# A queue of half tiles for block 1's weights, and two output copies of the first turn on GpSimd, in a transformer block on one core

## The chip, the core and the metric

The kernel runs on one core of one Trainium2 chip. The names of the engines are those of the profile: PE (TensorE matmul; PEld is its weight load), DVE (VectorE), ACT (ScalarE), POOL (GpSimd) and SP (SyncE, which here issues all DMAs, in order; its queue is written SPq). The metric is the device time of one execution in microseconds. Each engine works through its own instructions in order and waits on semaphores for those of others.

## The reference

One transformer block with adaptive layer norm, in float32: 2048 tokens of width 576, 32 heads of width 18, and a feed-forward layer 4608 wide.

```python
mod = (_silu(c) @ w_mod).reshape(c.shape[0], 6, 1, -1)
sa, ca, ga, sb, cb, gb = (mod[:, 0], ...)
h = _layernorm(x) * (1 + ca) + sa
x = x + ga * _A_ref(h, A_wqkv, A_wo)      # qkv, softmax(q k / sqrt(Dh)) v, @ wo
h = _layernorm(x) * (1 + cb) + sb
x = x + gb * _B_ref(h, B_w1, B_w2)        # silu(h @ w1) @ w2
```

## The kernel before

**Split numbers.** A float32 operand of a large product is kept as a high part, rounded to fp32r, and a low part, the rest; a product is three passes (high x high, and the two mixed ones). A weight tile therefore goes through GpSimd once: a cast makes the high part, a subtraction the low one, and the weights that a modulation gate scales (wo by ga, w2 by gb) are multiplied by it first.

**Stages.** The first layer norm and the q, k and v projections come first. Then attention goes over four blocks of 512 queries, each over 8 quads of four heads; one pass over the eight quads is called a turn here. For a quad, an estimate of each row's largest score is gathered from psa with DVE's mx (L755, L757), turned to mt (L777), written by SP to mscr (L782) and read back as two rows of qt (L786), so that the second scores, psb (L805), come out with the maximum subtracted; ACT makes pt from them (exponential, L807), and PE sums pt with v in psv (L842), which ACT evicts (ov, L846). out_b (L860 to L870) normalizes that on DVE and sends it with DMAs on SP to the output rows ou.

What follows attention in a block b runs in the next turn, cut into small pieces between the attention matmuls on PE (post(b); of the last block it runs alone at the end). o_T(kt) makes the split of ou: th (high, ACT, L923) and tl (low, GpSimd L926; for the half tile kt = 4 DVE, L928). proj multiplies by wo; then come the second layer norm, its transposes h_T, and the feed-forward layer in 36 tiles of 128, in chunks of four: mlp1 works on two w1 tiles at a time and ends in g (ACT) and its low part (GpSimd, L1072), mlp2 on four w2 tiles, for four groups of 128 tokens. Each result of proj and mlp2 is added to x in two halves: DVE adds the first, and the second goes over ACT into gt (L950, two buffers) and is added by GpSimd (L951).

**Weights.** Only block 1 (b = 0) splits weights. weights() loads a raw half tile from HBM (L672, three buffers), splits it on GpSimd (L674 to L676) and at its next call sends the finished tile to scratch memory (L665); the later blocks load that (L667). The calls stand where the list of pieces asks for them, as pieces without matmuls: prefetch for wo, w_load and w2_load for w1 and w2.

**Order.** PE's order is written out by the kernel: a loop of steps takes by turns a score matmul, a value matmul or the next piece of the filler (post's list), with a plan of when the other engines will be done (plan.t is its clock in ns, chain and plan.op book work on A, V or G), and an item's need holds it back until then. The other engines' order comes from a scheduler that follows the program's order; after_pe ties an instruction to PE's turn.

Of the kernel before, what the change touches and what calls it, by code (L numbers as in the profile page):

```python
# [60 lines left out]
PVMAX, PVMIN = 5, 3  # L61
QKB = 3
# [28 lines left out]
def f(ap):  # L91
    return ap.bitcast(F32)
# [247 lines left out]
def tile_adaln_block(ctx: ExitStack, tc: tile.TileContext, x, wqkv, wo, w1, w2, c, wfirst, wcol, out):  # L340
# [318 lines left out]
    stores = []  # L659

    def weights(w, src, scr, first, gate=None):

        while stores:
            w_, scr_ = stores.pop()
            nc.sync.dma_start(f(scr_), f(w_))  # L665
        if not first:
            nc.sync.dma_start(f(w), f(scr))  # L667
            return
        n = w.shape[2] // 2
        for cs in (slice(0, n), slice(n, 2 * n)):  # L670
            raw = mp["p"].tile([P, 320], F32, tag="raw", name="raw", bufs=3)[:, :n]
            nc.sync.dma_start(raw, src[:, cs])  # L672
            if gate is not None:
                nc.gpsimd.tensor_tensor(raw, raw, gate[:, cs], op=ALU.mult)  # L674
            nc.gpsimd.tensor_copy(w[:, 1, cs], raw)
            nc.gpsimd.tensor_tensor(w[:, 0, cs], raw, f(w[:, 1, cs]), op=ALU.subtract)  # L676
        stores.append((w, scr))
# [173 lines left out]
    def out_b(i, ov):  # L851
# [15 lines left out]
        chain([("V", 700), ("V", 260), ("V", 460), ("V", 700)], plan.t + 700, None, lambda at: o.update({("at", b): at + 5500}))  # L867
# [24 lines left out]
    def prefetch(b):  # L892
        pool = mp["p"]
        c = ready[b] = {}
        for kt in range(KT):
# [4 lines left out]
            weights(w, wo[:, kt, :], wos[kt], b == 0, ga)  # L900
# [6 lines left out]
    def post(b):  # L907
# [7 lines left out]
        def o_T(kt):  # L915
# [5 lines left out]
            chain([("A", 600)], plan.t, None, lambda at: o.update(th=at + 1500))  # L921
            n = P if kt < 4 else 64
            after_pe(nc.scalar.activation(hi[:n], src[:n], AF.Copy))  # L923
            eng = nc.vector if last and kt % 2 == 0 or kt == 4 else nc.gpsimd
# [5 lines left out]
        def proj(j, part):  # L930
            if part == 0:
                def ops(g, i):
                    kt, a, w = PASS[i]
                    return (c["tl"] if a else c["th"])[:, kt, j * P:(j + 1) * P], c["wo", kt][:, 1 - w, g * HH:(g + 1) * HH]

                c["pp"] = Pair([bank("psp", psA)[:, :HH] for _ in range(2)], ops, 14, not state["tail"])
# [85 lines left out]
        def w_load(i):  # L1022
            c["w1", i] = pool.tile([P, 2, KT * P], F32R, tag="w1", name="w1t", bufs=W1B)
            weights(c["w1", i], w1[i], w1s[i], b == 0)

        def w2_load(i):
            c["w2", i] = pool.tile([P, 2, D], F32R, tag="w2", name="w2t", bufs=5)
            weights(c["w2", i], w2[i], w2s[i], b == 0, gb)
# [15 lines left out]
        def mlp1(i, part):  # L1044
            if part == 0:
# [5 lines left out]

                c["p1"] = Pair([bank("ps1", psA) for _ in range(2)], ops, 14, not state["tail"], short=not last)
# [22 lines left out]
        def mlp2(i0, j, part):  # L1075
            if part == 0:
# [3 lines left out]

                c["p2"] = Pair([bank("ps2", psF)[:, :HH] for _ in range(2)], ops, 3 * CH, not state["tail"])
# [17 lines left out]
        fl.add(0, lambda: w_load(0))  # L1099
        fl.add(0, lambda: w_load(1))  # L1100
        fl.add(0, lambda: w2_load(0))
        if EARLY:
# [5 lines left out]
        def add_mlp1(i, w2n=()):  # L1108

            for part in range(NG):  # L1110
                fl.add(MMC * len(GR[not last][part]), lambda part=part: mlp1(i, part), need={0: pair_need, NG // 2: half_need}.get(part))
                for p_, n in w2n:
                    if p_ == part:
                        fl.add(0, lambda n=n: w2_load(n))
                if part in (0, 2) and i + 2 < NFT:
                    fl.add(0, lambda n=i + 2 + part // 2: w_load(n))

        def add_mlp2(i0, add):
            for j in range(NST):
                for part in range(len(G2)):  # L1120
                    add(MMH * len(G2[part]), lambda j=j, part=part: mlp2(i0, j, part), None, {0: pair_need, len(G2) // 2: half_need}.get(part))

        add_mlp1(0)
        for i0 in range(0, NFT, CH):
            if i0 + CH < NFT:
                add_mlp1(i0 + 2, [(NG // 2, i0 + 1)])
                add_mlp1(i0 + CH, [(0, i0 + 2), (0, i0 + 3)])
                add_mlp2(i0, fl.add)
                fl.add(0, lambda i=i0 + CH: w2_load(i))
            else:  # L1130
                add_mlp1(i0 + 2, [(1, i0 + 1), (2, i0 + 2), (3, i0 + 3)])
# [366 lines left out]
    while now < 2 * (total + LEAD) or pend or later:  # L1498
# [5 lines left out]
        run_later()  # L1504
        fill.free()
# [109 lines left out]
```

## Time and profile before

| | |
|---|---|
| runs, median (lowest to highest) | 2426.76 us (2426.68 to 2430.24) |
| the profiled execution: its own time, its span | 2421.15 us, 2419.3 us |
| PE busy | 2326.0 us, 96% |
| DVE busy | 1777.0 us, 73% |
| ACT busy | 1483.1 us, 61% |
| POOL busy | 629.8 us, 26% |
| mean granted clock of PE | 0.989 |

The profile is of one execution, which is why its time is not the median. A row of the profile names a line, an engine, an operation and out<-in, with the number of instructions and the time; in brackets stands how long the engine had been idle before, and what released it. The clock that PE is granted is given as a share of full speed. PE's share of 96% is an average over stages with different limits, so the prediction reads it turn by turn.

### The profile page before, as it was taken

Reading aid. Unit: us, or ns where it says so; the run is one execution under the profiler, and the core shown is the slowest. Engines: PE = TensorE matmul, PEld = TensorE weight load, DVE = VectorE, ACT = ScalarE, POOL = GpSimd, SP = SyncE. Lnnn points to the kernel's source line nnn. Section 1 sums busy time; section 2 is a strip of 40 time slices with the busy share of each in tenths; the row PEclk is TensorE's granted clock in tenths of the full one; section 3 lists DMA queues with packets and bytes.
Section 4 is the critical chain, followed back from the end, with each engine's and each line's share of the span. In section 5 each row is a group of like instructions: output and inputs, shape, how many; then the busy total and the mean of one; then the engine's idle time right before and its main releaser. Section 6 shows DMA issues by size and latency. Waiting matters only on the chain.

```text
span 2419.3 us, 52050 instructions
## 1 busy us (share of the span) xinstructions
PE 2326.0 (96%) x19844; PEld 1599.3 (66%) x19844; DVE 1777.0 (73%) x3110; ACT 1483.1 (61%) x2736; POOL 629.8 (26%) x766
## 2 busy tenths in 40 slices
PE   6999999998999999989999999999999999989999
PEld 4874444434567767666667677776676777678998
DVE  8768989886877778767887887888887887134333
ACT  5247777775666767666676776776776677722121
POOL 5201011113665665663211111112211111110000
PEclk9999999999999999999999999999999999999999
DMA  7455555454566666665555554554644554336563
GB/s 252 162 175 173 164 175 179 158 156 154 193 212 201 208 213 210 205 210 173 194 176 179 181 167 157 171 183 140 207 163 162 185 177 163 120 104 233 197 210 117
DMA packets 201472, 432.99 MB, mean 179 GB/s; under 512 B 31362, under 2 KB 67618, under 8 KB 201226
## 3 DMA queue, kind: packets, MB, share of 16 engines
q1 hardware_dynamic: 201226, 429.68, 53.9%
q8 instruction: 158, 2.59, 0.5%
q14 instruction: 88, 0.72, 0.1%
HBM read 338.54 MB, written 86.33 MB: 176 GB/s over the span
## 4 chain that ended last, share of the span: by engine, by line
PE 80%; DMA 6%; DVE 6%; POOL 3%; ACT 3%; issue 2%; SPq 0%; ACTq 0%; POOLq 0%; DVEq 0%
PE ps L485 23%; PE psv L842 17%; PE psa L755 12%; PE ps L479 10%; PE psb L805 8%; PE psqk L590 3%; DMA raw<-in_w 3%; DVE mx L757 2%; PE psv L485 2%; PE psp L485 1%; ACT pt L807 1%; PE psqk L485 1%; PE psv L1288 1%; POOL w1t L676 1%; PE psqk L1288 1%
## 5 line engine op out<-in xcount | busy, mean ns | idle before, releaser
L757 DVE TENSOR_REDUCE mx<-psa 128x1 f32<-128x512 f32 x2048 | 1321.3, 684 | 319.3 <-PE psb L805 168.8
L807 ACT ACTIVATE pt<-psb 128x512 f32<-128x512 f32 x2048 | 1131.6, 598 | 495.0 <-PE psb L805 306.5
L805 PE MATMUL psb<-qt,kb 56*128 56x512 f32 x2048 | 753.7, 425 | 37.8 <-ACT pt L807 23.9
L755 PE MATMUL psa<-ka,qt 54*128 54x512 f32 x2016 | 699.6, 415 | 6.3 <-DVE mx L757 5.2
L755 PEld LDWEIGHTS psa<-ka,qt 54*128 54x128 f32 x2016 | 337.0, 186 | 293.2 <-DVE mx L757 196.2
L842 PE MATMUL psv<-pt,vt 128*32 128x512 f32 x4096 | 512.7, 604 | 2.3 <-ACT ov L846 1.7
L485 PE MATMUL ps<-w2t,g 64*128 64x288 f32 x4992 | 413.8, 295 | 2.5 <-ACT gt L950 2.4
L805 PEld LDWEIGHTS psb<-qt,kb 56*128 56x128 f32 x2048 | 354.1, 185 | 85.9 <-ACT pt L807 56.4
L485 PEld LDWEIGHTS ps<-w2t,g 64*128 64x128 f32 x4992 | 386.9, 188 | 35.8 <-DVE mx L757 10.1
L485 PE MATMUL ps<-hh,w1t 64*128 64x512 f32 x1944 | 371.4, 394 | 2.6 <-DVE x L947 1.6
L485 PEld LDWEIGHTS ps<-hh,w1t 64*128 64x128 f32 x1944 | 220.6, 186 | 39.8 <-DVE mx L757 9.2
L842 PEld LDWEIGHTS psv<-pt,vt 128*32 128x32 f32 x4096 | 99.4, 109 | 215.8 <-issue 208.9
L1072 POOL TENSOR_TENSOR g<-etmp,g 128x512 fp32r<-128x512 f32 x108 | 137.9, 1298 | 393.9 <-ACT g L1071 336.2
L951 POOL TENSOR_TENSOR x<-x,gt 128x288 f32<-128x288 f32 x116 | 92.7, 801 | 408.6 <-ACT gt L950 408.6
L485 PE MATMUL ps<-hl,w1t 64*128 64x512 f32 x864 | 197.5, 392 | 0.6 <-POOL hl L412 0.6
L947 DVE TENSOR_TENSOR x<-ps,x 128x288 f32<-128x288 f32 x184 | 83.9, 456 | 124.4 <-PE ps L479 76.5
L479 PE MATMUL ps<-w2t,g 128*128 128x288 f32 x960 | 133.5, 299 | 7.4 <-ACT g L1071 5.9
L479 PEld LDWEIGHTS ps<-w2t,g 128*128 128x128 f32 x960 | 131.1, 191 | 9.9 <-ACT g L1071 6.3
L485 PEld LDWEIGHTS ps<-hl,w1t 64*128 64x128 f32 x864 | 105.3, 186 | 11.0 <-POOL hl L412 1.1
L1068 ACT ACTIVATE eq<-ps 128x512 f32<-128x512 f32 x36 | 21.6, 600 | 146.3 <-PE ps L479 146.3
L479 PE MATMUL ps<-hh,w1t 128*128 128x512 f32 x360 | 106.9, 390 | 0.5 <-DVE hh L414 0.5
L1069 DVE SCALAR_TENSOR_TENSOR etmp<-etmp 128x512 f32<-128x512 f32 x108 | 77.1, 747 | 22.9 <-ACT etmp L1068 22.3
(144 smaller groups left out, 2076.6 us busy)
## 6 DMA issues: line engine op xcount, KB each, us to landing
w1t<-w1s SPq DMA_DIRECT2D x108, 640.0 KB
w2t<-w2s SPq DMA_DIRECT2D x108, 576.0 KB
kb<-kscr SPq DMA_DIRECT2D x512, 108.0 KB
ka<-kscr SPq DMA_DIRECT2D x504, 108.0 KB
w1s<-w1t SPq DMA_DIRECT2D x36, 640.0 KB
w2s<-w2t SPq DMA_DIRECT2D x36, 576.0 KB
vt<-vscr SPq DMA_DIRECT2D x32, 608.0 KB
qt<-qscr SPq DMA_DIRECT2D x128, 108.0 KB
```

Source lines behind the costliest of these rows:

```text
L479: mm(self.ps[late], lhsT=lhsT, rhs=rhs, start=(i == 0), stop=(i == self.n - 1))
L485: done = mm(self.ps[g], lhsT=lhsT[rows], rhs=rhs[rows], start=(s == 0), stop=(s == self.end))
L590: mm(qk_ps[0], lhsT=w[b][:, kt, :], rhs=(hTl if a else hTh)[:, kt, n * 512:(n + 1) * 512], start=(i == 0), stop=(i == 13))
L755: mm(ps, lhsT=t["q"][64 * j:64 * j + 54, hp, stt * P:(stt + 1) * P], rhs=t["a" if ("a", kc, hp) in t else "b", kc, hp][64 * j:64 * j + 54, ...
L757: return lambda: nc.vector.tensor_reduce(t["mx"][:, 2 * j + hp, stt, kc:kc + 1], ps, axis=AX.X, op=ALU.max)
L805: state["pe"] = mm(ps, lhsT=t["b", kt // 4, hp][64 * e:64 * e + 56, kt % 4 * P:(kt % 4 + 1) * P], rhs=t["q"][64 * e:64 * e + 56, hp, :], s ...
L807: nc.scalar.activation(t["P"][kt, hp][:, e, :], ps, AF.Exp, scale=SCALE)
L842: mm(t["ps"][32 * h:32 * h + 32, :], lhsT=t["v"][:, c0:c0 + 32], rhs=t["P"][kt, h // 2][:, h % 2, :], start=(kt == 0), stop=(kt == NKT - 1 ...
L947: nc.vector.tensor_add(c["x1"][j][:, hs], ps, c["x1"][j][:, hs])
L951: nc.gpsimd.tensor_add(c["x1"][j][:, hs], c["x1"][j][:, hs], t)
L1069: nc.vector.scalar_tensor_tensor(t, t, 1.0, u, op0=ALU.add, op1=ALU.mult)
L1072: (nc.vector if last else nc.gpsimd).tensor_tensor(g[:, 1, :], t, f(g[:, 0, :]), op=ALU.subtract)
```

## The change

weights() no longer loads and splits in block 1. It enters an ask in a queue, a w1 tile ahead of w2 tiles of which nothing has been loaded. serve(), called once per step of the main loop, does at most one store, one split of a half and one load of a half: a load when fewer than three halves are under way and 1500 ns (w1) or 2000 ns (gated) of the plan have passed since the last, a split when 5000 ns have passed since its load, a store 4000 ns after the tile's second split. Load and split are tied to PE's turn. settle() makes what is still missing before the first matmul that reads it.

The requests are moved: four w1 tiles, and in block 1 four w2 tiles too, stand right behind the projection (before two and one), and later ones a few parts further on in mlp1 and mlp2. In block 1's o_T the casts of kt = 3 and 4 and the low part of kt = 4 go to GpSimd, and the plan's time at which ou has landed is put 1000 ns later.

```diff
+EACH, LAND, STORE = (1500, 2000), 5000, 4000
...
-    stores = []
-    def weights(w, src, scr, first, gate=None):
-        while stores:
-            w_, scr_ = stores.pop()
-            nc.sync.dma_start(f(scr_), f(w_))
+    asks, flight, stores = [], [], []
+    last_load = [0]
+    def weights(key, w, src, scr, first, gate=None):
         if not first:
             nc.sync.dma_start(f(w), f(scr))
             return
-        n = w.shape[2] // 2
-        for cs in (slice(0, n), slice(n, 2 * n)):
-            raw = mp["p"].tile([P, 320], F32, tag="raw", name="raw", bufs=3)[:, :n]
-            nc.sync.dma_start(raw, src[:, cs])
-            if gate is not None:
-                nc.gpsimd.tensor_tensor(raw, raw, gate[:, cs], op=ALU.mult)
-            nc.gpsimd.tensor_copy(w[:, 1, cs], raw)
-            nc.gpsimd.tensor_tensor(w[:, 0, cs], raw, f(w[:, 1, cs]), op=ALU.subtract)
-        stores.append((w, scr))
+        ask = {"key": key, "w": w, "src": src, "scr": scr, "gate": gate, "n": w.shape[2] // 2, "at": 0, "halves": [0, 1]}
+        i = len(asks)
+        while key[0] == "w1" and i and asks[i - 1]["key"][0] == "w2" and len(asks[i - 1]["halves"]) == 2:
+            i -= 1
+        asks.insert(i, ask)
+    def load_half():
+        ask = asks[0]
+        h, n = ask["halves"].pop(0), ask["n"]
+        raw = mp["p"].tile([P, 320], F32, tag="raw", name="raw", bufs=3)[:, :n]
+        after_pe(nc.sync.dma_start(raw, ask["src"][:, h * n:h * n + n]))
+        flight.append((plan.t, ask, h, raw))
+        last_load[0] = plan.t
+        if not ask["halves"]:
+            asks.pop(0)
+    def split_half():
+        _, ask, h, raw = flight.pop(0)
...
+        if gate is not None:
+            after_pe(nc.gpsimd.tensor_tensor(raw, raw, gate[:, cs], op=ALU.mult))
+            nc.gpsimd.tensor_copy(hi, raw)
+        else:
+            after_pe(nc.gpsimd.tensor_copy(hi, raw))
+        nc.gpsimd.tensor_tensor(w[:, 0, cs], raw, f(hi), op=ALU.subtract)
+        if h:
+            stores.append((plan.t + STORE, w, ask["scr"]))
...
+    def serve():
+        if stores and stores[0][0] <= plan.t:
+            store_one()
+        if flight and flight[0][0] + LAND <= plan.t:
+            split_half()
+        if asks and len(flight) < 3 and last_load[0] + EACH[asks[0]["gate"] is not None] <= plan.t:
+            load_half()
...
-        chain([...], plan.t + 700, None, lambda at: o.update({("at", b): at + 5500}))
+        chain([...], plan.t + 700, None, lambda at: o.update({("at", b): at + (5500 if b else 6500)}))
...
             n = P if kt < 4 else 64
-            chain([("A", 600)], plan.t, None, lambda at: o.update(th=at + 1500))
-            after_pe(nc.scalar.activation(hi[:n], src[:n], AF.Copy))
-            eng = nc.vector if last and kt % 2 == 0 or kt == 4 else nc.gpsimd
+            if b == 0 and kt > 2:
+                o["th"] = plan.t + 2200 * (kt - 2)
+                after_pe(nc.gpsimd.tensor_copy(hi[:n], src[:n]))
+            else:
+                chain([("A", 600)], plan.t, None, lambda at: o.update(th=at + 1500))
+                after_pe(nc.scalar.activation(hi[:n], src[:n], AF.Copy))
+            eng = nc.vector if last and kt % 2 == 0 or b and kt == 4 else nc.gpsimd
...
-        fl.add(0, lambda: w_load(0))
-        fl.add(0, lambda: w_load(1))
+        for i in range(4):
+            fl.add(0, lambda i=i: w_load(i))
         fl.add(0, lambda: w2_load(0))
+        if b == 0:
+            for i in range(1, 4):
+                fl.add(0, lambda i=i: w2_load(i))
...
             if i0 + CH < NFT:
-                add_mlp1(i0 + 2, [(NG // 2, i0 + 1)])
-                add_mlp1(i0 + CH, [(0, i0 + 2), (0, i0 + 3)])
-                add_mlp2(i0, fl.add)
-                fl.add(0, lambda i=i0 + CH: w2_load(i))
+                w2s_ = [(0, w2_load, i0 + 1), (4, w2_load, i0 + 2), (9, w2_load, i0 + 3)] if i0 or b else []
+                if i0 == 0:
+                    w2s_ += [(1, w_load, 4), (3, w_load, 5)]
+                add_mlp1(i0 + 2, *w2s_)
+                add_mlp1(i0 + CH, (6, w_load, i0 + 6), (11, w_load, i0 + 7))
+                add_mlp2(i0, fl.add, (2, w_load, i0 + 8), (9, w_load, i0 + 9), (18, w2_load, i0 + 4))
...
         run_later()
+        serve()
         fill.free()
```

**How the instructions move.** In the rows below stand line, operation, out<-in, the tile's size and, behind an x, a count; a number behind a name tells tiles of one name apart and differs between the kernels. First GpSimd, around the adds to x in a second-layer chunk of the second turn (in which block 1's post-attention work runs); before:

```order
L1072 TENSOR_TENSOR g<-etmp,g 128x512 x2
L676 TENSOR_TENSOR w1t<-raw,w1t 128x320
L675 CAST w1t<-raw 128x320
L674 TENSOR_TENSOR raw<-raw,gb 128x288
L676 TENSOR_TENSOR w1t<-raw,w1t 128x320
L674 TENSOR_TENSOR raw<-raw,gb 128x288
L951 TENSOR_TENSOR x_6582<-x_6582,gt 128x288
L674 TENSOR_TENSOR raw<-raw,gb 128x288
L951 TENSOR_TENSOR x_6584<-x_6584,gt 128x288
```

and with the change:

```order
L1125 TENSOR_TENSOR g<-etmp,g 128x512 x2
L695 CAST w1t<-raw 128x320 x2
L696 TENSOR_TENSOR w1t<-raw,w1t 128x320 x2
L1003 TENSOR_TENSOR x_6528<-x_6528,gt 128x288
L695 CAST w1t<-raw 128x320
L696 TENSOR_TENSOR w1t<-raw,w1t 128x320
L695 CAST w1t<-raw 128x320
L696 TENSOR_TENSOR w1t<-raw,w1t 128x320
L695 CAST w1t<-raw 128x320
L696 TENSOR_TENSOR w1t<-raw,w1t 128x320
L1003 TENSOR_TENSOR x_6530<-x_6530,gt 128x288
```

Before, raw halves of w2 are multiplied by the gate right ahead of each x add. With the change whole splits (cast, subtract) stand there, those of halves that SP loads further ahead.

Second SP, around one quad's max row in the second turn, mscr and its reload qt; before:

```order
L665 DMA w1s<-w1t 128x1280
L672 DMA raw<-in_w 128x288 x2
L665 DMA w1s<-w1t 128x1280
L672 DMA raw<-in_w 128x320
L724 DMA kb_84<-kscr 54x512 x2
L724 DMA ka_83<-kscr 54x512 x2
L724 DMA kb_85<-kscr 54x512 x2
L665 DMA w2s<-w2t 128x1152
L672 DMA raw<-in_w 128x320
L782 DMA mscr<-mt 128x32
L672 DMA raw<-in_w 128x320
L786 DMA qt<-mscr 2x32x32 x2
```

and with the change:

```order
L703 DMA w1s<-w1t 128x1280
L679 DMA raw<-in_w 128x320
L771 DMA kb_86<-kscr 54x512 x2
L771 DMA ka_83<-kscr 54x512
L771 DMA kb_87<-kscr 54x512
L703 DMA w1s<-w1t 128x1280
L771 DMA ka_83<-kscr 54x512
L679 DMA raw<-in_w 128x320
L771 DMA kb_87<-kscr 54x512
L829 DMA mscr<-mt 128x32
L679 DMA raw<-in_w 128x320
L833 DMA qt<-mscr 2x32x32 x2
```

The rows keep their mixture: a raw load stands between mscr and the reload in both, and the stores of finished tiles (w1s, w2s) come a few places further ahead of mscr.

Third the first turn's output copies. On ACT before:

```order
L807 ACTIVATE pt_2038<-psb 128x512 x2
L807 ACTIVATE pt_2030<-psb 128x512 x2
L807 ACTIVATE pt_2031<-psb 128x512 x2
L923 ACTIVATE th<-ou 128x512
L923 ACTIVATE th<-ou 64x512
L807 ACTIVATE pt_2032<-psb 128x512 x2
L807 ACTIVATE pt_2033<-psb 128x512 x2
```

and on GpSimd with the change:

```order
L693 CAST wo_6527<-raw 128x288
L977 TENSOR_TENSOR tl<-ou,th 128x512 x3
L696 TENSOR_TENSOR wo_6527<-raw,wo_6527 128x288
L971 CAST th<-ou 128x512
L971 CAST th<-ou 64x512
L977 TENSOR_TENSOR tl<-ou,th 128x512
L979 TENSOR_TENSOR th<-ou,th 64x512
```

The two th copies have left ACT's exponentials (pt), and stand on GpSimd with the subtractions behind them, the last of which (th<-ou,th) was DVE's.

43 lines of the change are left out of this document (31 added, 12 removed).

## The prediction

> **What bounds the kernel now.** I split the span at the last evictions of output quads 8, 16, 24 and 32, which bound the second to fourth turn over the eight head quads, and read each stretch (columns: window, its length, then busy us and count of PE, PEld, DVE, ACT and POOL, granted PE clock, DMA share, GB/s):
>
> ```profile
> 564.30:1119.50 555.20, 519.92 (x4816) 361.85 (x4816) 423.57 (x713) 360.58 (x661) 329.43 (x455) 0.97 0.61 198
> 1119.50:1631.10 511.60, 506.85 (x5008) 362.86 (x5004) 418.97 (x720) 362.21 (x667) 93.96 (x94) 1.00 0.53 176
> 1631.10:2130.80 499.70, 494.37 (x4804) 343.62 (x4806) 351.95 (x611) 347.78 (x644) 93.03 (x93) 1.00 0.48 160
> ```
>
> All three are bound by PE (94, 99 and 99% busy). The first of them, the second turn, in which block 1's post-attention work runs and its weights are split, has PE idle for 555.2 - 519.9 = 35.3 us, against 4.8 and 5.3 in the others, and a clock under 1.00. Only that excess can be won; the change leaves the later two in their order. So I looked next for the half-clock stretches of the second turn, and for the PE instructions that stood idle before them:
>
> ```profile
> 577.70:587.90 10.20, 3.69 (x15) 1.59 (x17) 2.36 (x3) 3.31 (x6) 1.26 (x1) 0.50 0.51 177
> 704.00:707.30 3.30, 3.30 (x29) 3.30 (x26) 1.18 (x2) 1.25 (x3) 1.34 (x2) 0.50 0.33 108
> 762.00:765.30 3.30, 3.30 (x28) 3.30 (x26) 1.76 (x3) 1.40 (x3) 2.14 (x3) 0.50 0.60 197
> 874.70:878.00 3.30, 3.30 (x27) 3.30 (x27) 1.95 (x3) 1.59 (x3) 2.85 (x5) 0.50 0.60 200
> 973.60:980.40 6.80, 5.54 (x25) 1.98 (x27) 0.44 (x1) 1.00 (x2) 5.99 (x7) 0.50 0.58 184
> 1045.30:1052.10 6.80, 4.59 (x31) 4.62 (x33) 1.44 (x3) 1.68 (x3) 2.60 (x5) 0.50 0.40 124
> ...
> 584.21 1.27 PE L805 MATMUL psb<-qt,kb 56*128 56x512 f32 x2 [9.07 <-ACT pt L807]
> 703.02 0.50 PE L805 MATMUL psb<-qt,kb 56*128 56x512 f32 x1 [2.70 <-ACT pt L807]
> 760.35 0.50 PE L805 MATMUL psb<-qt,kb 56*128 56x512 f32 x1 [1.19 <-ACT pt L807]
> 815.72 0.50 PE L805 MATMUL psb<-qt,kb 56*128 56x512 f32 x1 [0.87 <-ACT pt L807]
> 872.92 0.53 PE L485 MATMUL ps<-w2t,g 64*128 64x288 f32 x4 [2.36 <-ACT gt L950]
> 974.86 0.76 PE L805 MATMUL psb<-qt,kb 56*128 56x512 f32 x1 [4.85 <-issue]
> 1047.51 1.09 PE L805 MATMUL psb<-qt,kb 56*128 56x512 f32 x2 [6.86 <-DMA qt<-mscr]
> ...
> PE psb L805 <- issue: 6.3, 2, 4.8
> ```
>
> Six half-clock stretches, each beside one of these stalls; half of a stretch is lost. (The last row says that a second stall of the sixth one's kind was 6.3 - 4.85 = 1.5.) They have three causes.
>
> **A, the first turn's output copies.** ACT holds two th copies that wait for the transfer of ou, and its exponentials queue behind them:
>
> ```profile
> 582.24 0.63 ACT L923 ACTIVATE th<-ou 128x512 fp32r<-128x512 f32 x1 [8.36 <-DMA ou<-ov]
> ```
>
> PE stood 9.07 at 584.21; with 10.2 / 2 = 5.1 of clock that is **14.2 us**.
>
> **B, splits ahead of the x adds.** The stalls at 703, 760, 816 and 873 are one chain: GpSimd waits for a raw half tile to land, behind it stands the x add, behind that ACT's gt eviction (two gt buffers), behind that PE:
>
> ```profile
> 870.88 0.79 POOL L674 TENSOR_TENSOR raw<-raw,gb 128x288 f32<-128x288 f32 x1 [1.61 <-DMA raw<-in_w]
> 871.63 0.79 POOL L951 TENSOR_TENSOR x<-x,gt 128x288 f32<-128x288 f32 x1
> ...
> ACT gt L950 <- POOL x L951: 16.2, 5, 4.7
> ```
>
> 2.70 + 1.19 + 0.87 + 2.36 = 7.1 of idle, and three stretches of 3.3 / 2 = 5.0: **12.1 us**.
>
> **C, late max rows.** SP issues its DMAs in order, and waits for GpSimd's splits before raw loads and stores (the second turn's rows, the last one the third's):
>
> ```profile
> SPq L672 <- POOL w1t L676: 70.9, 25, 5.9
> SPq L665 <- POOL w1t L676: 33.2, 30, 3.9
> SPq L786 <- DMA mscr<-mt: 26.5, 8, 5.4
> SPq L665 <- POOL w2t L676: 24.8, 20, 4.2
> ...
> SPq L786 <- DMA mscr<-mt: 16.8, 8, 3.6
> ```
>
> The first, second and fourth sum to 128.9 us. What queues behind them is a quad's max row, which goes out to mscr and back as two rows of qt before that quad's next scores may run:
>
> ```profile
> 955.86 0.21 DVE L777 STREAM_TRANSPOSE mt<-ms 128x32 f32<-128x32 f32 x1
> 965.64 1.07 SPq L782 DMA_DIRECT2D mscr<-mt  x1
> ...
> 1026.86 0.21 DVE L777 STREAM_TRANSPOSE mt<-ms 128x32 f32<-128x32 f32 x1
> 1038.72 0.34 SPq L782 DMA_DIRECT2D mscr<-mt  x1
> 1044.49 1.38 SPq L786 DMA_DIRECT2D qt<-mscr  x2
> ```
>
> mt was ready 965.64 - 956.07 = 9.6 and 1038.72 - 1027.07 = 11.7 us before its store was issued; the stalls that followed were 4.85 and 6.86, each about 4.8 shorter than the lateness. So a store on time ends them. Sum: 4.85 + 1.5 + 6.86 = 13.2, and 2 x 6.8 / 2 = 6.8: **20.0 us**.
>
> **The change part by part.** *o_T.* The copies of kt 3 and 4 leave ACT for GpSimd, the kt-4 subtraction leaves DVE for it. GpSimd's rows of the second turn (count | busy us, mean ns | idle before), with its longest wait for a raw half and a stretch of 60 us for PE's pace:
>
> ```profile
> L676 POOL TENSOR_TENSOR w1t<-raw,w1t 128x320 fp32r<-128x320 f32 x72 | 63.4, 892 | 0.2
> L676 POOL TENSOR_TENSOR w2t<-raw,w2t 128x288 fp32r<-128x288 f32 x72 | 59.4, 837 | 0.4
> L674 POOL TENSOR_TENSOR raw<-raw,gb 128x288 f32<-128x288 f32 x72 | 59.4, 825 | 80.8 <-DMA raw<-in_w 80.2 <-PE psb L805 0.4
> L1072 POOL TENSOR_TENSOR g<-etmp,g 128x512 fp32r<-128x512 f32 x34 | 43.5, 1297 | 0.3 <-ACT g L1071 0.3
> L675 POOL CAST w1t<-raw 128x320 fp32r<-128x320 f32 x72 | 33.7, 476 | 80.0 <-DMA raw<-in_w 61.2 <-PE ps L485 11.7 <-PE psb L805 4.8
> L675 POOL CAST w2t<-raw 128x288 fp32r<-128x288 f32 x72 | 30.2, 442 | 18.8 <-PE ps L485 18.2
> ...
> L990 POOL CAST h<-etmp 128x512 fp32r<-128x512 f32 x1 | 0.6, 612 | 0.0
> ...
> POOL raw L674 <- DMA raw<-in_w: 80.2, 54, 5.2
> ...
> 840.00:900.00 60.00, 57.64 (x541) 42.48 (x540) 45.89 (x76) 39.29 (x73) 40.07 (x54) 0.97 0.63 205
> ```
>
> Two casts at 0.61, one subtraction already there and one new (each 1.30, by the 512-column row of g) make 3.8 us behind the landing, where ACT, POOL and DVE shared them before. The wait for the landing stays, but on GpSimd, behind which only block 1's weights queue; ACT goes on with exponentials, and the plan gives the projection 1 us more. Bounds: nothing of the stall left (gain 14.2), or PE short of other work for the 9.07 less the pt matmuls it can now feed (gain 5). I keep 3 of idle and one short stretch (1.7), since the projection still starts after the same transfer: gain **9.5**.
>
> *The queue.* No matmul, byte or GpSimd operation is dropped: a w1 half costs 0.476 + 0.892 = 1.37 us, a gated w2 half 0.825 + 0.442 + 0.837 = 2.10, before as after. What moves is when. In the two listings of the instructions' order a split's first operation now stands a median of 43 PE instructions behind its raw load's place, before 12; at 60.00 us for 541 of them that is 4.8 us against 1.3, near the longest landing wait above (5.2). So the 80.2 + 61.2 us in which GpSimd waited for landings mostly go, and with them the engine's lateness on which B hangs: x adds stand behind splits whose data are there. Bounds 0 to 12.1 (a loss is rival 2's); I take **11**, leaving one short wait.
>
> SP in turn waits for GpSimd only where a raw buffer or a store asks too early: a raw load is issued by the plan's clock, at most three halves under way, a store 4 us behind its split by the plan. That takes most of the 128.9 us out of SP's queue. But one raw load still stands between mscr and its reload in four of eight quads, and a w1 or w2 store a few places ahead of mscr. Bounds 0 to 20.0; I leave 4 for one late row: **16**.
>
> *What comes closer.* The second-layer weights of the first chunk go right behind the projections: 8 x 1.37 + 8 x 2.10 = 27.8 us of GpSimd against loads spaced 8 x 1.5 + 8 x 2.0 = 28. It is hidden by LN2, whose GpSimd work is small; uncovered, each us is one of PE. And weights are ready later: w1 tile 5's last subtraction stands 18 PE instructions (2.0 us) ahead of its first matmul, before 94 or more; the last w2 half of a typical chunk 56 to 61 (6.2 to 6.8 us), before 165 or more. Bounds 0 (all on time) to 8 chunks times several us (rival 2); I take one stall of 1.8 with a 3.3-us stretch at half speed, **-3.5**, for the tightest of them. The small waits of the turn that hang on the same queues give +1.
>
> Sum: 9.5 + 11 + 16 - 3.5 + 1 = **34**. The profiled execution took 2421.15, so 2387 there; it lies 2426.76 - 2421.15 = 5.6 under the median of the runs, so the predicted time is 2393.
>
> [...]
>
> **Rivals.** (1) *The max rows stay late.* Their transfers, not SP's waits, may hold them: mscr took up to 5.4 us to land against 3.6 in the third turn, behind weight stores and raw loads that all stay, in part in the same places. Against it: the lateness of 9.6 and 11.7 was before the issue. If 12 of C's 16 stay lost, the gain is 22: 2405.
>
> [...]
>
> (2) *Weights come too late: slower.* In the 6.2 to 6.8 us that the last w2 half has, GpSimd may have a w1 half (1.37), two g subtractions (1.30 each) and the half itself (2.10) to do: 6.1. The margin is nil, so a raw half that lands r late is r of PE in each of eight chunks, with some 1.7 of clock. At r = 2.6 the 8 x 4.3 = 34 eat the gain; at the longest landing wait, 5.2, they cost 55: 2427 + 21 = 2448. For it: all chunks share the pattern. Against it: the split is placed after the planned landing, g and splits rarely meet at once, and GpSimd has 555 - 329 = 226 us free.
>
> (3) *Throughput, not order, is the limit*, and the stalls only move: no change, 2427. Against it: GpSimd was busy 59% and DMA 61%.
>
> **How the numbers follow.** Forecast (gain 24 to 46, 2381 to 2403) 0.60; rival 1 (2403 to 2415) 0.18; rival 2 0.16; rival 3 0.06. 46 is A, B and C whole. About 0.2% (4.9 us) is what a measurement here can tell from no change. Faster is the first two and a third of rival 3: 0.80; same 0.04; slower 0.16. The range of eight in ten runs from 2380 up to the milder end of rival 2, at r = 1.5 and its clock, 8 x 3.2 = 26 against 34, which is 2419, and a little beyond: 2422.
>
> **What would show it.** A: no idle over 3 us near the start of the second turn, ACT without a th copy there, GpSimd waiting for ou. B: no ACT gt behind a POOL x of over 1 us. C: SP's waits for GpSimd below 40 us, mscr within 2 us of mt, no psb waiting for qt. Rival 1: mscr on time but landing over 5 us later. Rival 2: PE's layer matmuls waiting for w2t or w1t subtractions at the chunks. The second turn should shrink from 555.2 to about 521, the next two stay within 2 us. I am wrong if the turn's half-clock stretches stay near six, or a new wait repeats by the chunk.

## The result and the profile after

The change made the kernel faster, by less than half of what was forecast: 2412.47 us median (2407.57 to 2414.7, 4 runs) against 2427.97 (2426.68 to 2430.24), a ratio of 0.9932, 95% interval [0.9914, 0.9951]; run again on another chip, 0.9952 [0.9933, 0.9972]. The forecast was 34 us, measured are 15.5. The profiled execution took 2407.57 us, 13.6 less than that of before.

The windows of the three turns with the change (columns as in the prediction), bounded by the same evictions:

```profile
563.70:1095.20 531.50, 512.76 (x4816) 355.90 (x4816) 423.60 (x712) 359.57 (x658) 330.81 (x449) 0.99 0.63 204
1095.20:1615.70 520.50, 509.46 (x5008) 365.23 (x5004) 418.38 (x720) 362.49 (x667) 101.92 (x106) 0.99 0.53 177
1615.70:2117.30 501.60, 496.24 (x4804) 343.81 (x4804) 351.94 (x612) 347.60 (x643) 93.11 (x93) 1.00 0.48 160
```

The second turn is 555.2 - 531.5 = 23.7 us shorter, but the third is 520.5 - 511.6 = 8.9 longer, and the fourth 1.9. A turn that I took as untouched pays part of the bill: the last chunk's waits, below, lie in it. The PE instructions that stood idle longest, from the timeline:

```profile
580.28 0.53 PE L486 MATMUL psp<-wo,th 64*128 64x288 f32 x4 [1.84 <-POOL th L971]
582.40 0.61 PE L486 MATMUL psp<-wo,tl 64*128 64x288 f32 x2 [1.59 <-POOL tl L977]
...
606.86 0.49 PE L802 MATMUL psa<-ka,qt 54*128 54x512 f32 x1 [1.80 <-DVE mx L804]
...
662.88 0.50 PE L486 MATMUL ps<-hh,w1t 64*128 64x512 f32 x2 [1.18 <-POOL w1t L695]
666.53 0.77 PE L486 MATMUL ps<-hh,w1t 64*128 64x512 f32 x1 [3.14 <-POOL w1t L696]
...
1108.74 0.53 PE L486 MATMUL ps<-w2t,g 64*128 64x288 f32 x4 [2.00 <-POOL w2t L696]
1112.28 0.61 PE L486 MATMUL ps<-w2t,g 64*128 64x288 f32 x2 [3.00 <-POOL w2t L693]
```

The old stalls are gone. New ones wait for GpSimd at three places: the output copies (580), w1 tiles 4 and 5 (663 to 667), and the last chunk's w2 (1109 to 1112). Behind each of them stands a stretch at half clock:

```profile
581.30:588.00 6.70, 5.10 (x35) 4.76 (x37) 1.29 (x2) 1.08 (x2) 2.31 (x2) 0.50 0.26 88
666.60:669.90 3.30, 3.30 (x16) 2.65 (x18) 1.09 (x2) 0.60 (x2) 3.17 (x3) 0.50 0.72 293
1110.40:1117.10 6.70, 4.56 (x32) 4.24 (x34) 1.36 (x2) 1.08 (x2) 2.62 (x4) 0.50 0.43 172
```

Where B and C had been, PE stood idle for 8.8 and 12.1 us before the change (first view), and for 0.5 and 2.9 with it (second):

```profile
690.00:905.00 215.00, 206.18 (x1942) 146.77 (x1938) 164.42 (x271) 142.01 (x260) 134.26 (x187) 0.98 0.63 205
955.00:1085.00 130.00, 117.90 (x1115) 84.21 (x1114) 92.65 (x151) 80.35 (x147) 79.77 (x109) 0.95 0.63 206
```

```profile
690.00:890.00 200.00, 199.50 (x1961) 143.91 (x1959) 165.33 (x272) 142.23 (x261) 128.56 (x177) 1.00 0.65 212
940.00:1060.00 120.00, 117.11 (x1141) 84.33 (x1139) 95.59 (x156) 83.03 (x152) 82.56 (x111) 1.00 0.68 219
```

Since both kernels leave 19844 PE records in nearly the same order, the start of the n-th of them can be compared. The table gives it for this and later runs, in us against the profile of before (negative is earlier), each counted from its own 3450th, because starts drift by a few us ahead of the second turn, as SP's loads of qt at 567.42 us in the full change and at 570.76 in "w1 first, no front" show (the text calls the n-th record the n-th matmul):

```
n-th PE record            3500   3700   4200   4300   8300   8700    last
before, at us            554.8  594.6  658.3  671.9 1111.8 1154.4
full change               -0.6   -3.6   -0.4   +4.9  -24.3  -15.3   -13.5
full change again         -0.6   -2.5   -1.5   +6.3  -23.8  -13.8   -14.1
copies only               -0.6   +0.4   +5.9   +5.9   +0.3   +1.4    +1.6
queue only                -0.6   -1.3   -1.4   +6.5  -22.3  -13.5   -11.1
first chunk later         -0.6   -2.4   -1.6   +6.3  -18.1   -9.2    -7.6
last chunk fast           -0.6   -4.0   -1.1   +6.6  -22.2  -21.0   -21.0
w1 asked first            -0.6   -2.1   -0.6   +3.6  -26.3  -25.1   -24.9
w1 first, no front        -0.6   -2.8   -2.2   -2.7  -27.4  -25.3   -21.6
new places, no queue      -0.6   +1.0   +7.6   +7.1   -5.3   -5.4    -4.8
no landing time           -0.6   -8.2   -7.2   -7.5  +82.3  +93.0   +94.7
store at once             -0.6   -6.2   -0.5   -0.8  -19.4  -17.7   -16.6
queue, old places         -0.6   -2.2   +0.4   +0.6 +134.3 +141.0  +142.6
w1 first, no copies       -0.6   -1.8   -0.6   -0.8  -25.2  -24.0   -21.4
wo at once                -0.6   -9.1   -7.4   -7.5  -34.1  -32.2   -28.4
wo at once, no copies     -0.6   -5.3   -2.4   -2.7  -27.1  -25.9   -24.1
w1 first, again           -0.6   -2.3   -1.3   -1.2  -26.8  -24.6   -24.6
```

Columns 3500 to 4200 hold term A and the layer norm, 4200 to 4300 the wait for w1, 4300 to 8300 terms B and C, 8300 to 8700 the last chunk. With the change: A +0.2 (forecast -9.5), w1 +5.2, B and C -29.2 (-27), the last chunk +9.0; the forecast had +3.5 for all that comes closer, and -1 for small waits. Two terms are wrong; the sum of B and C is not. The 6700th matmul (931.0 us before) lies between B's stalls and C's two long ones: up to it -16.1 of the 29.2 had come, behind it -13.1.

### The profile page after: what moved, and what is told of

It is laid out like the page before. It is cut to its first block, busy times and chain, and to the rows that moved or that the text cites. A ratio compares the mean times of both kernels' runs of the same rounds, so it can differ in the third digit from the quotient of the medians.

```text
span 2405.8 us, 52151 instructions
## 1 busy us (share of the span) xinstructions
PE 2323.4 (97%) x19844; PEld 1596.2 (66%) x19844; DVE 1775.2 (74%) x3109; ACT 1482.1 (62%) x2734; POOL 637.5 (26%) x769
## 4 chain that ended last, share of the span: by engine, by line
PE 84%; DVE 7%; DMA 4%; ACT 3%; POOL 2%; issue 1%; SPq 0%; ACTq 0%; POOLq 0%; DVEq 0%
PE ps L486 25%; PE psv L889 18%; PE psa L802 13%; PE ps L480 10%; PE psb L852 8%; PE psqk L591 3%; DVE mx L804 3%; PE psp L486 2%; PE psv L486 2%; DMA raw<-in_w 1%; ACT pt L854 1%; PE psqk L486 1%; PE psv L1350 1%; PE psqk L1350 1%; PE psp L480 1%
```

## The experiments

Their times (median us, and the ratio to the kernel before on the same chip):

| run | median | ratio, 95% interval |
|---|---|---|
| copies only | 2429.94 | 1.0022 [1.0009, 1.0035] |
| queue only | 2415.14 | 0.9965 [0.9952, 0.9977] |
| first chunk later | 2419.07 | 0.9972 [0.9963, 0.9981] |
| last chunk fast | 2405.65 | 0.9921 [0.9906, 0.9936] |
| full change again | 2413.24 | 0.9952 [0.9933, 0.9972] |
| w1 asked first | 2401.15 | 0.9897 [0.9877, 0.9917] |
| w1 first, no front | 2399.91 | 0.9890 [0.9864, 0.9917] |
| new places, no queue | 2421.50 | 0.9983 [0.9967, 0.9998] |
| no landing time | 2518.61 | 1.0381 [1.0359, 1.0404] |
| store at once | 2401.70 | 0.9907 [0.9889, 0.9925] |
| queue, old places | 2568.85 | 1.0594 [1.0576, 1.0613] |
| w1 first, no copies | 2400.50 | 0.9885 [0.9865, 0.9906] |
| wo at once | 2396.43 | 0.9884 [0.9870, 0.9898] |
| wo at once, no copies | 2398.67 | 0.9894 [0.9878, 0.9909] |
| w1 first, no front, again | 2402.58 | 0.9908 [0.9894, 0.9922] |

"No front" means that the first chunk's w2 tiles 1 to 3 are not asked for right behind the projection; "no copies" means without the o_T edit. "W1 first, no copies" and the two runs "wo at once" have no front either.

### The two halves of the change

The kernel before with the new lines of o_T alone, and the full change with the old ones (the lines are those of the diff ahead of the prediction):

```diff
-            eng = nc.vector if last and kt % 2 == 0 or kt == 4 else nc.gpsimd
+            if b == 0 and kt > 2:               # copies only; queue only is this reversed
+                after_pe(nc.gpsimd.tensor_copy(hi[:n], src[:n]))
...
+            eng = nc.vector if last and kt % 2 == 0 or b and kt == 4 else nc.gpsimd
```

> The kernel before with the o_T edit alone (th copies of kt 3 and 4 and the kt-4 subtraction on GpSimd, the plan's times with it). Theory: PE no longer stands 9.07 us for pt, but what it wins is some 3 us at 595 us of the profile and goes again in the layer norm behind it (waits for DVE and for the projection's operands), so that from about 660 us on PE is level with the kernel before: within 1.5 us there, and a time within 2 us of before. Rival: the copies are worth what I forecast (9.5 us) and it was the queue's later weights that took it back in the full change: then PE is 5 to 10 us ahead at 660 us and the time is that much shorter.

> The full change without its o_T edit. Theory: the 9.07-us stall and its slow clock are back near 580 us, PE is some 3 us behind the full change at 595 us, but level with it (within 1.5 us) from 670 us on; the time is that of the full change within 2 us. Rival (the copies are worth 9.5): 5 to 10 us longer than the full change throughout.

Neither theory had the first right: alone, the copies made the kernel slower, by 0.2%. PE is not ahead at all at the 3700th matmul and 5.9 us behind at the 4200th. DVE's waits there, from its timeline, point at the cause:

```profile
619.21 0.46 DVE L961 BATCH_NORM_STATS2 st<-x 128x6 f32<-128x288 f32 x1 [2.73 <-POOL x L955]
622.35 0.35 DVE L393 TENSOR_TENSOR t<-r 128x1 f32<-128x1 f32 x1 [2.24 <-POOL r L387]
```

In that timeline GpSimd's x add and r of the layer norm stand behind splits; PE then waits 3.25 us for DVE's mx, and a stretch of 10.2 us at half clock follows. In the kernel before and in the full change DVE waits there 0.2 us or less for x and 1.3 for r, in "new places, no queue" 2.8 and 2.6. So the waits come where the copies stand on GpSimd and there is no queue. The second went about as the theory said: with the queue, the copies' place changes the 4200th matmul by 1.1 us (in favour of the old place). Its ratio, 0.9965 [0.9952, 0.9977], overlaps the full change's second one and lies just above its first. The queue and its places carry the gain; whether the copies add something to it, 2.4 to 3.0 us at the last matmul, is not settled by these runs.

### The two late weights

```diff
-                w2s_ = [...] if i0 or b else []          # first chunk later: as for other chunks,
-            for i in range(1, 4):                         # and not behind the projections
-                fl.add(0, lambda i=i: w2_load(i))
+                w2s_ = [...]
```

> The full change with the first chunk's w2 tiles 1 to 3 asked for in mlp1(2) like those of the other chunks, not right behind the projections. Theory: it is GpSimd's backlog of eight gated halves that makes w1 tiles 4 and 5 late, so the waits for w1t near 661 to 666 us (1.18 + 3.14 and 3.4 us at half clock) fall under 1 us in all, and the time is 4 to 6 us shorter than the full change. Rival: it is the place of the ask (w1 5's last subtraction now stands 4 PE instructions ahead of its first matmul, in the full change 18), so the wait stays at 3 us or more, or grows.

```diff
+        late = lambda key: key[0] == "w2" and key[1] > NFT - CH
-        if flight and flight[0][0] + LAND <= plan.t:
+        if flight and flight[0][0] + (3500 if late(flight[0][1]["key"]) else LAND) <= plan.t:
...
-... last_load[0] + EACH[asks[0]["gate"] is not None] <= plan.t:
+... last_load[0] + (1000 if late(asks[0]["key"]) else EACH[...]) <= plan.t:
```

> The full change with the last chunk's w2 tiles 33 to 35 served faster: loads at least 1000 ns apart (2000), splits 3500 ns behind their load (5000). Theory: these halves are only paced too slowly, so PE's waits for w2t near 1107 to 1113 us (2.00 + 3.00) fall under 1.5 us in all, the 6.8 us at half clock behind them go, and the time is 7 to 9 us shorter than the full change. Rival: it is GpSimd's other work in that place (four tl subtractions of the third turn, 5.0 us, and two of g, 2.6): the waits stay within 1.5 us of what they were.

> The full change, unchanged, beside the variants of this batch on one chip. Expected: 0.993 of before within 0.002, and the same two waits for late weights (near 661 to 666 us and 1107 to 1113 us of the profile), 14 us in all with their slow clock.

"First chunk later" was a miss, and its rival held: the wait for w1 is 7.9 us in the table, in the full change 5.2 and, run again, 7.8. That second run of the full change had both waits again, 17.7 us in the table, and its 0.9952 is just outside what was expected. "Last chunk fast" was a hit: the waits of 2.00 and 3.00 became one of 1.31, the slow stretch went, and the last chunk's 9.0 became 1.2. Pace had made those halves late; GpSimd's tl and g did not. Then both for w1:

```diff
-                    w2s_ += [(1, w_load, 4), (3, w_load, 5)]
+                    w2s_ += [(0, w_load, 4), (0, w_load, 5)]      # and late() is true for w1 4 and 5 too
```

> The full change with the last chunk's faster serving and with w1 tiles 4 and 5 asked for at part 0 of mlp1(2) (1 and 3) and served as fast (loads 1000 ns apart, splits 3500 ns after). The last subtraction of w1 5 stands 32 PE instructions ahead of its first matmul (18). Theory (place and pace of the ask decide): the waits for w1t near 662 us, 4.3 to 6.2 us in the runs so far, fall under 2 us, 4 to 7 us shorter than the run with the last chunk's faster serving alone. Rival (GpSimd's backlog of gated halves decides): SP still waits for a raw buffer, the wait stays above 3 us.

> The run before with, in addition, the first chunk's w2 tiles 1 to 3 asked for in mlp1(2), behind w1 4 and 5. Now neither place nor backlog should hold w1 4 and 5. Theory: the wait for w1t is under 1.5 us, as short as in the run before or shorter; what may come in its place are waits for w2t at the first chunk's mlp2, 1 to 3 us. Rival (backlog): only this run, and not the one before, loses the wait.

The wait fell to 4.2 us in the table and then to none (-2.2 to -2.7). Under 2 us had been expected of the first of the two, so its theory was a miss, and the backlog, the rival in both, held. Without the backlog but with w1 asked for at its old place ("first chunk later") the wait was 7.9. So place and backlog both held w1: in the full change PE stood ready at 662.88 - 1.18 = 661.7 and 666.53 - 3.14 = 663.4, and the raw loads had gone out only some 2.5 us before. SP's rows, then GpSimd's, of its timeline:

```profile
659.11 0.39 SPq L679 DMA_DIRECT2D raw<-in_w  x1
660.94 0.36 SPq L679 DMA_DIRECT2D raw<-in_w  x1
...
662.38 0.45 POOL L695 CAST w1t<-raw 128x320 fp32r<-128x320 f32 x1 [1.02 <-DMA raw<-in_w]
665.20 0.46 POOL L695 CAST w1t<-raw 128x320 fp32r<-128x320 f32 x1 [2.37 <-DMA raw<-in_w]
```

Without both late weights the time is 2399.91 beside 2413.24 for the full change on the same chip: 13.3 us, of the 14.2 and 17.7 that the table gives to them in its two executions.

### What wins B and C

The full change with weights() of before and no serve():

```diff
-    asks, flight, stores = [], [], []          # and load_half, split_half, store_one, serve, settle
+    stores = []                                # weights() loads and splits where it is called
```

> The full change with its moved requests and its o_T edit, but with the weights() of before: loads and splits where they are asked for, no queue. Theory (queue order wins B and C): the waits of ACT gt for POOL x and of psb for qt or issue stay, 8 us or more of PE idle between 690 and 1060 us, and the time is that of before or longer (0.998 to 1.006). Rival (the moved requests win them): PE gains 15 us or more over before between 690 and 1060 us.

The run "w1 first, no front" with LAND 0, and with STORE 0:

```diff
-EACH, LAND, STORE = (1500, 2000), 5000, 4000
+EACH, LAND, STORE = (1500, 2000), 0, 4000      # no landing time
+EACH, LAND, STORE = (1500, 2000), 5000, 0      # store at once
```

> The run with w1 asked first and no front, but LAND 0: a split stands right behind its load in the program, so GpSimd waits for each landing, as before the change; loads are spaced as they were. Theory (term B hangs on where the split stands to its landing): ACT's gt waits for POOL x again (over 5 us in all in the second turn, in the full change none), PE loses 5 to 12 us of term B between 695 and 880 us of the profile, and the time is 5 to 12 us longer than with LAND. Rival (B was won by the spacing of loads or by the moved requests): no loss over 2 us.

> The same run with STORE 0 (4000): SP gets a tile's store in the step after its second split and waits for GpSimd there. Theory (term C hangs on what SP waits for ahead of mscr): the max rows leave 3 us or more later than with STORE 4000 in at least two quads, and one or both of the waits of psb near 970 and 1040 us come back, 4 to 15 us. Rival (SP's waits for stores were never ahead of mscr; raw loads and their spacing decide): within 2 us of the run with STORE 4000.

The full change's queue with the requests of before:

```diff
-        for i in range(4):
-            fl.add(0, lambda i=i: w_load(i))
+        fl.add(0, lambda: w_load(0))
+        fl.add(0, lambda: w_load(1))            # and the places in mlp1 and mlp2 as before
```

> The full change's queue and o_T edit, with the requests at the places they had before. The last subtractions then stand 4 PE instructions (w1) and 13 (w2) ahead of their first matmuls in every chunk, where the full change has 94 and 56 to 61. Theory (lateness in PE instructions decides): PE waits for w1t or w2t subtractions in most chunks, 2 to 6 us each time with some slow clock, 30 to 80 us in all, and the time is above before. Rival (splits are in fact done well ahead, the order's distance says little): within 5 us of the full change.

Places without the queue win 12.4 of B and C's 29 us (7.1 to -5.3), which lies between the theory and its rival. Nearly all of it is B: at the 6700th matmul PE had won 11.8, behind it 0.6. PE still waits 6.0 us for qt, whose max row leaves 11.7 us late as it did before, and 3.2 for gt. So the moved requests win most of B, and C needs the queue. LAND 0 loses far more than expected, 119 us. The waits of GpSimd and SP in its second turn (565 to 1215 us) close a circle:

```profile
POOL raw L692 <- DMA raw<-in_w: 140.3, 34, 11.7
POOL w1t L695 <- DMA raw<-in_w: 80.8, 30, 7.4
...
SPq L703 <- POOL w2t L696: 158.9, 32, 8.4
SPq L703 <- POOL w1t L696: 87.1, 33, 6.2
```

GpSimd waits for a landing, SP for GpSimd's split before it may store, the next raw load stands behind that store, and GpSimd waits for it. The split's distance from its load is what keeps the queue from being worse than no queue. C hangs on it too: in this run six of the max rows leave 6.5 to 16.5 us late, and PE's waits for qt and issue are back (8.2 and 6.6 us).

STORE 0 was a miss: its ratio overlaps that with 4000, and the two late max rows leave 5.8 and 6.6 us behind mt, with 4000 5.5 and 6.5. Its profile, of an execution 6.5 us above the median of its runs, shows 18.6 us for B and C, where "w1 first, no front" and its second run have 24.7 and 25.6. But of these 6 to 7 us 4.9 are lost between the 4300th and the 4500th matmul (in the other two 2.3 and none); behind the 6700th it wins 10.9, the others 12.6 and 13.5. So the store's delay is worth some 2 us of C at most.

The last run went the way of its theory, at 143 us nearly twice the top of its price: with subtractions 4 and 13 PE instructions ahead, PE waits at nearly every chunk (565 to 1265 us):

```profile
PE ps L486 <- POOL w2t L693: 72.9, 19, 9.6
PE ps L486 <- POOL w2t L696: 15.4, 18, 2.7
PE ps L486 <- POOL w1t L696: 13.6, 11, 4.1
PE ps L486 <- POOL w1t L695: 11.2, 8, 3.7
```

### The output copies

> The run with w1 asked first and no front, without the o_T edit (ACT and DVE make the copies, the plan's times as before). Theory (what the copies win is lost again in the layer norm behind them, late weights or not): the stall of 8 to 9 us near 580 us is back, PE is 1 to 3 us behind that run at 595 us, but within 1.5 us of it at 658 us, and the time is within 3 us of it (2397 to 2403 beside a kernel before of 2425). Rival (the copies are worth what I forecast, and the late weights hid it): 5 to 10 us longer than that run from 595 us to the end.

```diff
-            if b == 0 and kt > 2:                 # o_T and the plan's times as before
-                o["th"] = plan.t + 2200 * (kt - 2)
-                after_pe(nc.gpsimd.tensor_copy(hi[:n], src[:n]))
```

The theory held, just outside two of its bounds (8 and 1.5 us): a wait of 7.37 us is back, PE is 1.0 us behind at the 3700th matmul and 1.6 at the 4200th, and the ratios are 0.9885 without the copies and 0.9890 with them. But one run spoke against its reason. With LAND 0 PE stood 8.2 us ahead at the 3700th matmul and kept 7.2 at the 4200th, so the layer norm does not take everything back. What differs there is when SP issues ou's transfer, 573.56 - 572.21 = 1.4 us after the transpose that makes ov. This transpose and the transfer in the kernel before (with all that SP issued between them), in the full change and in "wo at once":

```profile
568.83 0.70 DVE L865 STREAM_TRANSPOSE ov<-ou 128x512 f32<-128x512 f32 x1
569.54 1.83 SPq L714 DMA_DIRECT2D qt<-qscr  x4
571.78 0.34 SPq L731 DMA_DIRECT2D vt<-vscr  x1
572.22 0.38 SPq L665 DMA_DIRECT2D wos<-wo  x1
573.11 1.60 SPq L672 DMA_DIRECT2D raw<-in_w  x2
574.81 0.99 SPq L724 DMA_DIRECT2D ka<-kscr  x2
576.42 5.03 SPq L870 DMA_DIRECT2D ou<-ov  x5
```

```profile
568.18 0.70 DVE L912 STREAM_TRANSPOSE ov<-ou 128x512 f32<-128x512 f32 x1
572.52 4.99 SPq L917 DMA_DIRECT2D ou<-ov  x5
```

```profile
573.40 0.70 DVE L913 STREAM_TRANSPOSE ov<-ou 128x512 f32<-128x512 f32 x1
574.46 4.42 SPq L918 DMA_DIRECT2D ou<-ov  x5
```

From ov's end it is 6.9, 3.6 and 0.4 us. In the 6.9 us SP issues ten other DMAs, which takes 5.1; for GpSimd it waits 0.4. Before that, to 566.04, it had stood 1.9 us for a split of wo. "Wo at once" has this edit:

```diff
-... (3500 if late(flight[0][1]["key"]) else LAND)
+... (3500 if late(flight[0][1]["key"]) else 0 if flight[0][1]["key"][0] == "wo" else LAND)
```

> The run with w1 asked first and no front, with LAND 0 for wo's halves alone, which stand ahead of the first turn's last output transfers on SP. Theory (SP's late issue of ou's transfer sets the stall): the five transfers start 1.5 to 3 us sooner after ov than in the run without it (3.8 us), PE's waits for th and tl near 580 us (4.4 us in all, with a slow stretch) fall under 2.5 us, PE stands 3 to 6 us further ahead at the 3700th matmul and keeps at least half of it at the 4200th; the time is 2 to 6 us shorter. Rival (the layer norm gives it back): further ahead at the 3700th, level within 1 us at the 4200th, the same time within 2 us.

> The same without the o_T edit. Theory (the landing, not the engine that copies, sets the stall): PE's wait for pt near 580 us, 7.4 us in the run without the copies, shrinks by what the transfers start sooner, 1.5 to 3 us, and the time stays within 3 us of the run with the copies. Rival (with the transfer on time the copies' place is what is left): 4 us or more longer than with the copies.

> The run with w1 asked first and no front again, as the comparison on this chip: 0.989 of before within 0.003.

The theory held, a little beyond its bounds. The waits for th and tl fall from 4.8 us (2.53, 1.63 and 0.60 in the comparison's profile) to 0.82 in all, PE is 9.1 us ahead at the 3700th matmul and 7.4 at the 4200th (the comparison 2.3 and 1.3), and the time is 2396.43 beside 2402.58, 6.2 us shorter. Without the copies the transfer goes out 0.1 us after ov's end, and PE's wait for pt falls from 7.37 to 3.02. "Wo at once" has the lowest median and ratio of the study, 0.9884 [0.9870, 0.9898] of before, though "w1 first, no copies" on another chip is level with it by the ratio. Whether the copies' place is worth something then is not settled: 4.9 us at the 4200th matmul of one execution, 2.2 us by the medians, with ratios that overlap.

## Why the forecast missed

**B and C: right in their sum, with some luck.** The stalls that I named are gone: ACT's gt waits 0.3 and 0.2 us behind splits, where it was 16.2 for POOL x, PE has no wait for qt, and the two late quads' max rows leave sooner. B's three half-clock stretches went with its stalls (granted clock 1.00 in the second view of the stretches above), so they hung on idles of 1.19 to 2.70 us. But B's part came to 16.1 us (forecast 11; a stall of 1.5 in it was counted with C) and C's to 13.1 (16), and these errors cancel. From mt to the store's issue, in the two quads whose stalls had been 4.85 and 6.86:

```profile
943.95 0.21 DVE L824 STREAM_TRANSPOSE mt<-ms 128x32 f32<-128x32 f32 x1
949.51 0.68 SPq L829 DMA_DIRECT2D mscr<-mt  x1
...
1011.12 0.21 DVE L824 STREAM_TRANSPOSE mt<-ms 128x32 f32<-128x32 f32 x1
1016.92 0.34 SPq L829 DMA_DIRECT2D mscr<-mt  x1
```

5.4 and 5.6 us, before 9.6 and 11.7. That is 0.6 and 0.8 more than the slack of 4.8 us read off the stalls, and no wait followed. This slack was no constant: a third row left 12.2 us late before the change (issued at 702.85), and its quad stood only the 1.5. Two of my signs were wrong all the same, these rows within 2 us of mt and SP's waits for GpSimd below 40 us, and so was the expectation that GpSimd's waits for landings mostly go:

```profile
SPq L703 <- POOL w2t L696: 39.7, 17, 4.9
SPq L679 <- POOL w2t L696: 37.2, 17, 5.1
SPq L703 <- POOL w1t L696: 21.1, 11, 4.5
SPq L679 <- POOL w1t L696: 20.9, 14, 2.9
...
POOL raw L692 <- DMA raw<-in_w: 57.2, 23, 7.8
POOL w1t L695 <- DMA raw<-in_w: 27.5, 18, 4.3
```

Of SP's waits 118.9 us are left; before they were 145.8, with a row of 16.9 (L672 for w2t) that the prediction left out. Of GpSimd's for landings 84.7 are left of 141.4. That what is left stands where less depends on it is argued, not shown. How the 29 divide was tried in part: the places alone win most of B and nothing of C, a split far enough behind its load is needed for both, and the store's delay matters little. What the spacing of the loads adds was not tried.

**Rivals.** Rival 1 (max rows stay late) and rival 3 (throughput) did not come; that the time fell into rival 1's band, 2403 to 2415, is chance. Rival 2 came in part, at two places instead of eight: with 56 to 61 PE instructions of margin the typical chunk waits 1 us or less, with the 18 of w1 tile 5 PE waits 4.3 and, in the second run, 6.4 us, and in the last chunk 5.0. The point from which lateness decides lies between, and its price was underestimated where it struck.

**The step "what comes closer" failed: -3.5 became -14.2.** It priced one stall, w1 tile 5 (5.2 us in the table), and left out the last chunk (9.0). There is no next chunk's mlp1 there between the requests for w2 and the mlp2 that reads it, so these weights too stand close to their use. And it took the 18 instructions, 2.0 us, as time in hand. They are a place in the order; the raw load that the subtraction waits for went out late, as place, pace and backlog together made it.

**The step "o_T" failed: -9.5 became +0.2.** It named ACT's two copies as the cause of the 9.07 us, took the transfer's landing as given, and moved the wait to GpSimd, where PE met it again at the projection. PE was 3.0 us ahead at the 3700th matmul, and the layer norm took that back; how is not shown. The late landing was the main cause: with the transfer on time and the copies still on ACT the wait is 3.02. The transfer was issued 6.9 us after its data were ready, because SP had ten other DMAs to issue first, with a wait for a split of wo ahead of them. That is the in-order queue of C again, though here more by what it issues than by what it waits for. It was not looked for in A because ov's end was not set beside SP's row. Nor was GpSimd's chain behind the landing free: from th's start to the last subtraction's end it takes 583.69 - 579.62 = 4.1 us.

**Smaller slips.** I counted half of each slow stretch as lost, but only work done in it is slowed: PE was busy 3.69 of 10.2 us at 577.7, so 1.85 were lost, not 5.1. In the stretches at 973.6 and 1045.3 it was 5.54 and 4.59 of 6.8, so 5.1 in all, not 6.8. And the second turn before had seven such stretches, not six: one of 3.4 us at 635.7 stands beside none of the stalls listed, and is still there with the change (635.9). A was 10.9 us and C 18.3, which makes the 29.2 measured nearly all that B and C held (30.4).

## What to carry to other kernels

When a wait ends with a transfer, set the time at which its data were ready beside the time of its issue before blaming the engine that stands idle: here the same in-order queue held two stalls that looked unlike. When work is moved closer to its use to take it off another path, list its margin at every place, the first and the last round above all, and count it from the load, not from the place in the order. Compare executions by the n-th instruction of the bounding engine; it shows a gain that is lost again a turn later, which the total hides.

## What the chip showed beyond that

The half-clock stretches of B stood behind idles of 1.19 to 2.70 us, and one stretch of another run behind shorter ones. In the run "w1 first, no copies" PE had been idle 0.49 and 0.97 us shortly before 620.3 us, and then worked without a gap through 10.2 us at half speed:

```profile
616.90:620.30 3.40, 1.95 (x16) 0.49 (x8) 3.33 (x9) 2.04 (x4) 2.67 (x6) 1.00 0.50 148
620.30:630.50 10.20, 10.20 (x36) 4.95 (x36) 6.12 (x13) 6.08 (x10) 4.57 (x7) 0.50 0.71 247
```

At 0.50 for 10.20 us 5.1 us of work were lost in it, yet PE was 1.0 us behind "w1 first, no front" at the 3700th matmul and 1.6 at the 4200th. So most of the loss was made good, probably because the layer norm's operands were awaited there anyway, which is not shown. And with the change the fourth turn had a slow stretch of 3.4 us at 1690.6 behind idles of 1.34 and 0.24 us, where the kernel before had idles of 1.34 and 0.23 and none.

How the granted clock goes with PE's busy share can be counted in the traces of the kernel before and of the full change, between 480 and 2100 us. Their 12 half-speed stretches there last 3.41 us (seven), 6.83 (four) and 10.24 (one), and in each trace the changes of the clock lie whole multiples of 3.41 us apart. I cut both traces into windows of 3.41 us, counted from one of these changes, and set PE's share in one window beside the clock in the next. Of 9 full-speed windows in which PE was busy less than half of the time, 8 were followed by one at half speed; of 12 with 50 to 70%, 4; of 905 with more, none. (PE's busy time is modelled, so the shares are rough.) In "w1 first, no front" half speed from 681.9 to 685.3 us came even behind 3.90 us in which PE was busy for 3.35. In the fourth turn both idles fell into one such window with the change (first view, 1.83 of 3.40 us busy), and before they were shared out between two windows (second view, 2.06 and 3.17):

```profile
1687.20:1690.60 3.40, 1.83 (x12) 0.97 (x12) 3.40 (x6) 1.10 (x3) 1.73 (x2) 1.00 1.01 404
1690.60:1694.00 3.40, 3.40 (x18) 0.59 (x16) 0.87 (x2) 0.29 (x1) 0.00 (x0) 0.50 0.61 243
```

```profile
1700.70:1704.10 3.40, 2.06 (x18) 1.37 (x18) 3.40 (x6) 1.58 (x3) 3.32 (x4) 1.00 1.01 409
1704.10:1707.50 3.40, 3.17 (x28) 1.21 (x26) 2.75 (x5) 1.20 (x2) 0.29 (x1) 1.00 0.82 326
```

Between 50 and 70% the share alone does not decide it in these two traces, and nearly the same idles cost a slow stretch in one of the two executions and nothing in the other.
